# A recording list scheduler with new queue costs, other warm-up matmuls, and scanned states stored with the chunk innermost

## The chip, the cores and the metric

The kernel runs on one core of one Trainium2 chip. The metric is the device time of one execution in microseconds (us), as the median of several runs. Times inside an execution come from one profiled run.

## The reference

Three blocks follow each other, all in float32 with an output of 4 x 768 x 384. The first is a gated linear attention with a decaying state, the second mixes tokens with two 768 x 768 matrices after a rotation, the third is a gated spatial unit.

```python
f = 1.0 / (1.0 + np.exp(-f_logit))
for t in range(S):
    state = f[:, :, t, :, None] * state + np.einsum('bhd,bhe->bhde', k[:, :, t], v[:, :, t])
    y[:, :, t] = np.einsum('bhd,bhde->bhe', q[:, :, t], state)
...
theta = x @ w_theta
zr, zi = x * np.cos(theta), x * np.sin(theta)
y = np.einsum('ts,bsd->btd', w_tok_r, zr) + np.einsum('ts,bsd->btd', w_tok_i, zi)
u = x + y
x = u + np.maximum(u @ w_ch, 0.0)
...
h = np.maximum(x @ w_in, 0.0)
u, v = h[..., :512], h[..., 512:]
v_n = (v - mean(v)) / np.sqrt(var(v) + 1e-06)
out = (u * (np.einsum('ts,bsd->btd', w_spatial, v_n) + b_spatial[None, :, None])) @ w_out
```

There are 4 batches of 8 heads; a head has 768 steps and 48 channels.

## The kernel before

**The attention** takes two heads at a time: a unit u is one batch's pair of heads, 16 units in all, four for each batch. A head's 768 steps are cut into 12 chunks of 64. For a third of a batch's channels `dense` (line 462) loads f, k and q as tiles of 128 channels x 768 steps, makes the running decay `icp` with a scan on VectorE, and scales k and q with it; there are 12 such thirds. The tile f has one buffer, k and q have two (BUFS, line 39), so the load of the next f waits for the scan of the last. `att_load` (505) moves a unit's k and q rows within the chip into KP and QA, and loads v from HBM into VN and, straight behind q's rows, into VS. `att_k` (494) transposes k on TensorE (tile pt) and ScalarE copies it to KT. `att_s` (551) makes the 64 x 64 scores of six chunks (tile psc), which VectorE masks into QA. `att_w` (527) makes each chunk's own state (tile pw); ScalarE copies it to ub (called cu for the first four units), VectorE scans over the chunks in cb, with the chunk innermost, and ScalarE copies the states before each chunk to VS. VS is stored with the channel innermost, so both of these copies write one element in every 12 or 48. `att_x` (571) multiplies QA (stationary) with VS (moving, 48 columns) into px, which ScalarE copies to X.

**The mixing** transposes X (`p1_xt`), makes theta (`p1_theta`, tile pth), sine and cosine (`p1_z`), accumulates over the token matrices (`p1_acc`, tile acc) and applies the channel matrix (`p1_h`, tile hh). The first batch's matrices come as float64: `single` (394) loads the words of a block to ws (two buffers), and ScalarE and VectorE make float32 of them: w_theta into ft, the channel matrix into wb and wc, the token matrices into tk. **The third block** (`p2_v`, `p2_u`, `p2_s`, `p2_o`) follows batch by batch.

**The order.** Up to the third block every instruction is recorded by `Eng` (325; the profile therefore shows line 333 for all of them), and `Plan` (86) sets the order on each engine: `schedule` (197) runs a list schedule with `cost` (95) for each instruction, and for a DMA an issue time and a transfer at one rate; it repeats this four times with priorities from latest starts, keeps the best, and binds the order of TensorE, VectorE, ScalarE, GpSimd (POOL) and the one DMA queue, SP. SP issues in order: a DMA that waits for its data holds those behind it. The estimates set the order alone; waits are by semaphores. On TensorE all matmuls of one `group` stand together.

**Warm-up.** `run` (1013) issues FILL = 10 identity matmuls at the start; `warm` (426) adds two matmuls of 128 columns, whose result nobody reads, behind each bank of transposes and of scores in the first batch (12 transposes' and 16 scores' fillers).

Of the kernel before, what the change touches and what calls it, by code (L numbers as in the profile page):

```python
# [10 lines left out]
F32 = mybir.dt.float32  # L11
# [28 lines left out]

FILL = 10

# [11 lines left out]

MODE, HOP, ISSUE, RATE, LAND, SLACK = 0.1, 0.11, 0.45, 330e3, 0.9, 0.05
ROUNDS = 4
# [29 lines left out]
class Plan:  # L86
# [8 lines left out]
    def cost(self, o, e, ins, out, src):  # L95
        n = max([b.n for b in out + src] or [0])
        k = type(ins).__name__
        if e == "A":
            if k == "InstActivation":
                return 0.19 + 0.84e-3 * n + (0.95e-3 * n if abs(out[0].step) > 4 and n > 100 else 0)  # L100
            return 1.28
        if e == "V":
            if o.name.startswith("tensor_tensor_scan"):
                return 0.16 + 2.07e-3 * n
            if o.name == "tensor_scalar":
                return 0.15 + 0.53e-3 * n
            if o.name == "reciprocal":
                return 0.22
            return 0.15 + 1.045e-3 * n
        if e == "G":  # L110
            return 0.1 + 0.8e-3 * n if o.name == "memset" else 0.8
        if e == "Q":
            return ISSUE
        m, r = out[0].rows, out[0].n
        o.mode = (src[-1].rows, m)
        if o.name == "transpose":
            return 0.109
        if src[0].dt == F32R:
            return max(r / 2.4 + 13.3, m / 1.2 + 2) / 1e3
        if m < P:  # L120
            return max(2 * r / 2.4, 54) / 1e3 + 0.004
        return max(2 * (2 * r / 2.4 + 2), 214) / 1e3

    def add(self, e, name, ins):
# [5 lines left out]
        o.cost = self.cost(o, e, ins, o.out, o.src)  # L130
        o.bytes = max([b.n * b.rows * 4 for b in o.out] or [0])
        o.blk = (self.blk if e == "T" and self.blk else -o.i) if e == "T" else None
        o.pri = o.i if self.pri is None else self.pri
# [63 lines left out]
    def schedule(self):  # L197
# [30 lines left out]
        for _ in self.units:  # L228
# [21 lines left out]
            for o in u:  # L250
# [15 lines left out]
                elif e == "Q":  # L266
                    t += o.cost
                    dma = max(dma, t + 0.5) + o.bytes / RATE
                    end[o] = dma + LAND
                else:  # L270
                    if o.func == "sin":
                        t += 0.1 + (1.28 if func != "sin" else 0)
                    func = o.func or func
                    t += o.cost
                    end[o] = t + HOP
# [78 lines left out]
class Kernel:  # L354
    def __init__(self, tc, a):
        self.tc, self.a, self.nc = tc, a, tc.nc
        nc = tc.nc
        self.last, self.ready = None, False
        self.tk, self.nb, self.xt = {}, B, []
        self.cold = True  # L360
        self.plan = Plan(tc)
        e = {"V": nc.vector, "A": nc.scalar, "G": nc.gpsimd, "T": nc.tensor, "Q": nc.sync}
        self.V, self.A, self.G, self.T, self.Q = (Eng(self.plan, e[n], n) for n in "VAGTQ")
# [61 lines left out]

    def warm(self, p, src):
        if self.cold:
            for _ in range(2):
                self.T.matmul(p[:, DM:512], lhsT=src[:, 0:P], rhs=src[:, 0:P], start=True, stop=True)


    def att_open(self, ctx):
# [12 lines left out]
        self.cw = a1.tile([P, S], F32, name="cw")  # L445
        self.VS = [a1.tile([P, 2, NC, D], F32, name=f"vs{i}") for i in range(2)]
        self.VN = [a1.tile([P, 2, NT, D], F32, name=f"vn{i}") for i in range(2)]
# [8 lines left out]
        for t in self.VS:  # L456
            G.memset(t[0:64, 0, 0, :], 0.0)
            G.memset(t[64:128, 1, 0, :], 0.0)
        self.dn, self.un = {}, {}
# [34 lines left out]
    def att_k(self, b, g):  # L494
        self.group()
        k = self.dn[3 * b + g]["k"]
        for n in range(0, NT, 3):
            p = self.bank("pt")
            for i in range(3):
                self.T.transpose(p[:, P * i : P * i + P], k[:, P * (n + i) : P * (n + i) + P], self.ident)  # L500
            self.warm(p, k)
            self.A.activation(self.KT[:, n : n + 3, P * g : P * g + P], p[:, 0:DM].rearrange("p (n d) -> p n d", n=3), AF.Copy)
# [24 lines left out]
    def att_w(self, u):  # L527
# [9 lines left out]
        A.activation(cb, self.KP[w2][:, None, S:].to_broadcast([P, D, NC]), AF.Copy)  # L537
        w = [self.bank("pw")[:, 0 : 6 * D].rearrange("p (n d) -> p n d", n=NT) for _ in range(2)]
        for n in range(NT):
# [3 lines left out]
        for s in range(2):  # L543
            A.activation(ub[:, :, s:NC:2].rearrange("p e c -> p c e"), w[s], AF.Copy)
        fl = lambda z: z.rearrange("p e c -> p (e c)")
        V.tensor_tensor_scan(fl(cb), fl(ub), fl(cb), 0.0, op0=ALU.add, op1=ALU.mult)
        for i in range(2):
            r = slice(64 * i, 64 * i + 64)
            A.activation(VS[r, i, 1:NC, :].rearrange("p c e -> p e c"), cb[r, :, 0 : NC - 1], AF.Copy)

    def att_s(self, u, g):
        self.group()
        V, T = self.V, self.T
        K, qa = self.KP[u % 2], self.QA[u % 2]
        ps = self.bank("psc")
        for c in range(6):
            cc = slice(C * (6 * g + c), C * (6 * g + c) + C)
            for i in range(2):
                r = slice(64 * i, 64 * i + 64)
                T.matmul(ps[64 - 64 * i : 128 - 64 * i, C * c : C * c + C], lhsT=K[r, cc], rhs=qa[i][r, cc], start=True, stop=True)  # L560
        self.warm(ps, K)
        for i in range(2):
# [8 lines left out]
    def att_x(self, u, g, X):  # L571
        self.group()
        A, T, pr = self.A, self.T, u % NP
        qa, VS = self.QA[u % 2], self.VS[u % 2]
        ps = self.bank("px")[:, 0 : 6 * D].rearrange("p (n i d) -> p n i d", n=3, i=2)
        for i in range(2):
            for c in range(6):
                cc = 6 * g + c
                T.matmul(ps[64 * (c % 2) : 64 * (c % 2) + 64, c // 2, i, :], lhsT=qa[i][:, C * cc : C * cc + C], rhs=VS[:, i, cc, :], start=True, stop=True)
        A.activation(X[:, 3 * g : 3 * g + 3, 96 * pr : 96 * pr + 96].rearrange("p b (i e) -> p b i e", i=2), ps, AF.Copy)  # L580
# [42 lines left out]
    def p1_xt(self, b, X, tb):  # L623
# [4 lines left out]
        xt = self.xt[-1][:, :, P * (tb % 3) : P * (tb % 3) + P]  # L628
        p = self.mm.tile([P, 512], F32, name="pt", tag="th", bufs=2)
        for j in range(NJ):  # L630
            T.transpose(p[:, P * j : P * j + P], X[:, tb, P * j : P * j + P], self.ident)
# [8 lines left out]
    def p1_theta(self, b, tb, terms):  # L640
        self.group()
        V, A = self.V, self.A
        p = self.mm.tile([P, 512], F32, name="pth", tag="th", bufs=2)[:, 0:DM]
        (self.mm1 if b < THETA1 else self.mm3)(p, terms)
        sn = self.c2.tile([P, 2, DM], F32, name="sn", tag="sn")
# [226 lines left out]
    def general(self, xg, x2):  # L872
# [9 lines left out]
        with tc.For_i(0, B * NP, 1) as i:  # L882
            self.last, self.ready, self.cold = None, False, False
            f, k, q = [g1.tile([P, S], F32, name=f"g{n}") for n in "fkq"]
# [128 lines left out]
    def run(self):  # L1013
# [36 lines left out]
        run(w)  # L1050
        self.cold = False
        sw = ExitStack()
# [47 lines left out]
def layout(inputs):  # L1100
# [5 lines left out]
    def heads(x):  # L1106
# [12 lines left out]
        "vu": c(v2.reshape(B * NP, 2, NT, P, D).transpose(0, 3, 1, 2, 4)),  # L1119
        "va": c(v2.reshape(B * NP, 2, NC, C, D).transpose(0, 1, 3, 2, 4)),  # L1120
        "wt": raw(c(inputs["moe_w_theta"])),
# [21 lines left out]
```

## Time and profile before

| | us |
|---|---|
| median of 3 runs | 670.17 (665.01 to 672.14) |
| the profiled execution | 669.65 |
| its span | 667.5 |
| TensorE matmul busy | 611.6 (92%) |
| VectorE busy | 425.6 (64%) |
| ScalarE busy | 360.5 (54%) |
| GpSimd busy | 31.4 (5%) |

The profiled execution lasts 2.15 us longer than its span, which runs from the first to the last recorded work. PE is TensorE, PEld its weight loads, DVE VectorE, ACT ScalarE, SP the DMA queue. A float32 matmul leaves two records, a float32r matmul one. A busy PE is not a PE at its peak: ends are modelled, and a record counts as busy at either clock.

### The profile page before, as it was taken

The page shows a single profiled execution, that of the slowest core. Times are in us where ns is not written, and L with a number is a line of the kernel's source. Part 1 is how long each engine was busy: PE and PEld are TensorE (multiplying, and loading weights), DVE is VectorE, ACT ScalarE, POOL GpSimd, SP SyncE. Part 2 cuts the span into 40 slices and gives each one's busy share as a digit, 9 for nine tenths or more (in the row PEclk, how much of TensorE's full clock was granted, in tenths as well). Part 3 has the DMA queues.
Part 4 walks back from the last instruction along what each step waited for, and adds up shares of the span by engine and source line. Part 5 has one row for each costly group of instructions (what it writes and reads, how often), then busy time and mean ns, then how long its engine had stood idle before and what let it go on. Part 6 is the DMA issues. An engine that isn't in the chain of part 4 may idle for free.

```text
span 667.5 us, 12718 instructions
## 1 busy us (share of the span) xinstructions
PE 611.6 (92%) x5116; PEld 560.2 (84%) x5116; DVE 425.6 (64%) x757; ACT 360.5 (54%) x637; POOL 31.4 (5%) x72
## 2 busy tenths in 40 slices
PE   4468898599999799999999999999999999999996
PEld 4467566486789798898899998999899989998996
DVE  3786698688787796786588534769355354517250
ACT  3676788654886766895578211644362255126211
POOL 5110001000001020000000000000000000000000
PEclk7778998689999899999999999999999999999999
DMA  8876854878857979536565953341102000010002
GB/s 266 207 211 207 268 188 156 251 251 259 306 161 233 304 211 302 184 126 208 183 202 176 303 190 89 112 130 38 72 0 72 36 35 25 1 66 7 1 1 76
DMA packets 40962, 102.04 MB, mean 153 GB/s; under 512 B 5696, under 2 KB 11840, under 8 KB 40896
## 3 DMA queue, kind: packets, MB, share of 16 engines
q1 hardware_dynamic: 40896, 101.15, 48.1%
q8 instruction: 42, 0.69, 0.4%
q14 instruction: 24, 0.20, 0.1%
HBM read 71.17 MB, written 20.45 MB: 137 GB/s over the span
## 4 chain that ended last, share of the span: by engine, by line
PE 63%; DMA 16%; DVE 8%; ACT 6%; issue 3%; SPq 2%; POOL 1%; ACTq 0%; DVEq 0%; POOLq 0%
PE acc L333 14%; PE pg L333 14%; PE po L333 7%; PE pu L333 6%; PE pv L333 6%; PE pth L333 5%; DMA qa<-q 3%; PE hh L333 3%; DMA ws<-tok_dram 3%; PE psc L333 3%; DMA wb<-wp_dram 3%; PE px L333 2%; PE pt L333 2%; SPq L333 2%; DVE icp L333 2%
## 5 line engine op out<-in xcount | busy, mean ns | idle before, releaser
L333 PE MATMUL acc<-tk,z 128*128 128x384 f32 x828 | 169.0, 356 | 0.0
L333 PEld LDWEIGHTS acc<-tk,z 128*128 128x128 f32 x828 | 144.2, 189 | 9.6
L333 PE MATMUL pg<-wp,vn 128*128 128x384 f32 x576 | 101.0, 335 | 0.7 <-ACT wp L333 0.7
L333 PEld LDWEIGHTS pg<-wp,vn 128*128 128x128 f32 x576 | 99.9, 188 | 1.3 <-ACT wp L333 1.3
L333 PEld LDWEIGHTS psc<-qa,kp 64*64 64x64 f32 x768 | 31.5, 159 | 25.7 <-issue 21.3
L333 PE MATMUL psc<-qa,kp 64*64 64x64 f32 x768 | 35.9, 249 | 18.2 <-DMA qa<-q 11.6
L333 ACT ACTIVATE gt<-g 128x384 fp32r<-128x384 f32 x32 | 16.8, 526 | 63.6 <-DVE g L333 63.6
L333 PE MATMUL pu<-x,wi 128*128 128x384 f32 x288 | 50.7, 334 | 0.0
L333 PE MATMUL po<-wo,gt 128*128 128x384 f32 x288 | 50.6, 336 | 0.0
L333 PEld LDWEIGHTS pu<-x,wi 128*128 128x128 f32 x288 | 50.1, 188 | 0.3
L333 PEld LDWEIGHTS po<-wo,gt 128*128 128x128 f32 x288 | 50.0, 188 | 0.0
L333 PE MATMUL pv<-wi,x 128*128 128x512 f32 x216 | 49.8, 390 | 0.0
L333 DVE TENSOR_TENSOR qa<-psc,mask 64x384 f32<-64x384 f32 x64 | 35.5, 555 | 21.2 <-PE psc L333 19.9
L333 PEld LDWEIGHTS pv<-wi,x 128*128 128x128 f32 x216 | 40.5, 188 | 8.2
L333 PE MATMUL hh<-uT,wc 128*128 128x384 f32 x216 | 41.8, 343 | 2.3 <-DVE sn L333 1.0
L333 DVE BATCH_NORM_STATS2 st<-vv 128x6 f32<-128x512 f32 x24 | 16.5, 691 | 42.4 <-ACT vv L333 42.4
L333 PEld LDWEIGHTS px<-vs,qa 128*64 128x64 f32 x768 | 28.6, 156 | 16.0 <-ACT vs L333 7.9
L333 PE MATMUL px<-vs,qa 128*64 128x48 f32 x768 | 31.6, 242 | 10.8 <-ACT vs L333 7.1
L333 PEld LDWEIGHTS hh<-uT,wc 128*128 128x128 f32 x216 | 37.1, 188 | 4.6 <-DVE sn L333 1.4
L333 ACT ACTIVATE ws<-ws 128x768 f32<-128x768 f32 (+2 forms) x28 | 20.3, 732 | 28.6 <-DMA ws<-wi_dram 11.7
L333 DVE TENSOR_TENSOR g<-pg,bs 128x384 f32<-128x384 f32 x32 | 17.7, 555 | 27.2 <-PE pg L333 27.2
L333 ACT ACTIVATE vs<-cb 64x528 f32<-64x528 f32 x24 | 27.7, 1154 | 11.5 <-DVE cb L333 11.3
(113 smaller groups left out, 938.1 us busy)
## 6 DMA issues: line engine op xcount, KB each, us to landing
tk<-tkp SPq DMA_DIRECT2D x48, 384.0 KB, 4.3
ws<-tok_dram SPq DMA_DIRECT2D x12, 768.0 KB, 6.5
tkp<-tk SPq DMA_DIRECT2D x20, 384.0 KB, 4.5
f<-f_dram SPq DMA_DIRECT2D x12, 384.0 KB, 4.8
k<-k_dram SPq DMA_DIRECT2D x12, 384.0 KB, 5.2
q<-q_dram SPq DMA_DIRECT2D x12, 384.0 KB, 6.2
vn<-vu_dram SPq DMA_DIRECT2D x16, 288.0 KB, 5.0
vs<-va_dram SPq DMA_DIRECT2D x32, 144.0 KB, 4.2
```

What stands on the lines that cost most here:

```text
L333: r = f(*a, **k)
```

## The change

Four things. The planner's DMA costs: issue 0.6 us (was 0.45), 310 GB/s (was 330), 160 GB/s for transfers to 96 partitions or fewer, 1.2 us to land (was 0.9). The fillers: 30 at the start and 20 ahead of the first scores, all identity matmuls, which the planner counts as free; the 28 of the first batch's transposes and scores are gone. VS is stored as channel by chunk, with the chunk innermost, so the two copies follow the scan's own order and `att_x` reads a moving operand with a step of 12 elements; v's copy in HBM is laid out to match. The planner's extra cost for strided copies on ScalarE is gone.

```diff
-FILL = 10
+FILL = 30
+WARM = {("s", 0, 0): 20}
...
-MODE, HOP, ISSUE, RATE, LAND, SLACK = 0.1, 0.11, 0.45, 330e3, 0.9, 0.05
+MODE, HOP, ISSUE, RATE, NARROW, LAND, SLACK = 0.1, 0.11, 0.6, 310e3, 160e3, 1.2, 0.05
...
-                return 0.19 + 0.84e-3 * n + (0.95e-3 * n if abs(out[0].step) > 4 and n > 100 else 0)
+                return 0.19 + 0.84e-3 * n
...
+        if len(src) == 2 and src[0].t == src[1].t:
+            return 0.0
...
+        o.rate = RATE if max([b.rows for b in o.out] or [P]) > 96 else NARROW
...
-                    dma = max(dma, t + 0.5) + o.bytes / RATE
+                    dma = max(dma, t + 0.5) + o.bytes / o.rate
...
-    def warm(self, p, src):
-        if self.cold:
-            for _ in range(2):
-                self.T.matmul(p[:, DM:512], lhsT=src[:, 0:P], rhs=src[:, 0:P], start=True, stop=True)
+    def warm(self, p, key):
+        for _ in range(WARM.get(key, 0)):
+            self.T.matmul(p[:, 0:P], lhsT=self.ident, rhs=self.ident, start=True, stop=True)
...
-        self.VS = [a1.tile([P, 2, NC, D], F32, name=f"vs{i}") for i in range(2)]
+        self.VS = [a1.tile([P, 2, D, NC], F32, name=f"vs{i}") for i in range(2)]
...
-            G.memset(t[0:64, 0, 0, :], 0.0)
-            G.memset(t[64:128, 1, 0, :], 0.0)
+            G.memset(t[0:64, 0, :, 0], 0.0)
+            G.memset(t[64:128, 1, :, 0], 0.0)
...
-            A.activation(ub[:, :, s:NC:2].rearrange("p e c -> p c e"), w[s], AF.Copy)
+            A.activation(ub[:, :, s:NC:2], w[s].rearrange("p n e -> p e n"), AF.Copy)
...
-            A.activation(VS[r, i, 1:NC, :].rearrange("p c e -> p e c"), cb[r, :, 0 : NC - 1], AF.Copy)
+            A.activation(VS[r, i, :, 1:NC], cb[r, :, 0 : NC - 1], AF.Copy)
...
-                T.matmul(ps[...], lhsT=qa[i][:, C * cc : C * cc + C], rhs=VS[:, i, cc, :], start=True, stop=True)
+                T.matmul(ps[...], lhsT=qa[i][:, C * cc : C * cc + C], rhs=VS[:, i, :, cc], start=True, stop=True)
...
-        "va": c(v2.reshape(B * NP, 2, NC, C, D).transpose(0, 1, 3, 2, 4)),
+        "va": c(v2.reshape(B * NP, 2, NC, C, D).transpose(0, 1, 3, 4, 2)),
```

The order changes at many places. The first shown is SP from the second load of f to the third. In names like f1 or k2 the digit is the third of the channels; in kp0, qa00, qa01 it is the buffer and the head of a unit; ws is a raw weight block. Before:

```order
L333 DMA f1_205<-f_dram 128x768
L333 DMA qa01_107<-q0_142 48x768
L333 DMA kp0_104<-k0_140 48x780 x2
L333 DMA qa00_106<-q0_142 48x768
L333 DMA kp1_105<-k0_140 32x780
L333 DMA qa10_108<-q0_142 32x768
L333 DMA ws_174<-wt_dram 128x768
L333 DMA ws_828<-wc_dram 128x768
L333 DMA k2_344<-k_dram 128x768
L333 DMA q2_346<-q_dram 128x768
L333 DMA f2_342<-f_dram 128x768
```

The same place in the change:

```order
L337 DMA f1_221<-f_dram 128x768
L337 DMA qa00_106<-q0_142 48x768
L337 DMA ws_174<-wt_dram 128x768
L337 DMA kp0_104<-k0_140 48x780 x2
L337 DMA qa01_107<-q0_142 48x768
L337 DMA kp1_105<-k0_140 32x780
L337 DMA qa10_108<-q0_142 32x768
L337 DMA ws_840<-wc_dram 128x768
L337 DMA f2_370<-f_dram 128x768
L337 DMA k2_372<-k_dram 128x768
L337 DMA q2_374<-q_dram 128x768
```

The third f moves ahead of the third k and q, and the weight block ws_174 moves ahead of the first unit's kp0 and qa01.

The second place is VectorE, from the scan over the first unit's chunks (cu0) to the third decay scan (icp from f2). Before:

```order
L333 SCALAR_TENSOR_TENSOR cu0_250<-cu0_250 128x576
L333 TENSOR_TENSOR q1_209<-q1_209,cw_99 128x768
L333 TENSOR_TENSOR qa00_106<-psc_283,mask_91 64x384
L333 TENSOR_TENSOR qa01_107<-psc_283,mask_91 64x384
L333 TENSOR_SCALAR ft2_173<-ws_174 128x384
L333 SCALAR_TENSOR_TENSOR ft2_173<-ws_174,ft2_173 128x384 x2
L333 TENSOR_SCALAR wb_827<-ws_828 128x384
L333 SCALAR_TENSOR_TENSOR wb_827<-ws_828,wb_827 128x384
L333 RECIPROCAL fs2_348<-f2_342 128x12
L333 SCALAR_TENSOR_TENSOR wb_827<-ws_828,wb_827 128x384
L333 SCALAR_TENSOR_TENSOR icp_98<-f2_342,one_95 128x768
```

In the change:

```order
L337 TENSOR_TENSOR k1_223<-k1_223,icp_98 128x768
L337 TENSOR_TENSOR icp_98<-cw_99,icp_98 128x768
L337 SCALAR_TENSOR_TENSOR cw_99<-icp_98,cw_99 128x768
L337 TENSOR_TENSOR q1_225<-q1_225,cw_99 128x768
L337 TENSOR_TENSOR qa00_106<-psc_249,mask_91 64x384
L337 TENSOR_TENSOR qa01_107<-psc_249,mask_91 64x384
L337 SCALAR_TENSOR_TENSOR cu0_284<-cu0_284 128x576
L337 TENSOR_TENSOR qa00_106<-psc_317,mask_91 64x384
L337 TENSOR_TENSOR qa01_107<-psc_317,mask_91 64x384
L337 RECIPROCAL fs2_376<-f2_370 128x12
L337 TENSOR_SCALAR wb_839<-ws_840 128x384
L337 SCALAR_TENSOR_TENSOR icp_98<-f2_370,one_95 128x768
```

Two steps of the weight conversion wb go behind the third decay scan, and the k and q of the second third go ahead of the unit's masks and scan.

The third place is TensorE at the sixth unit (kp_105, vs_101) in the second batch's attention, at the end of its scores. Before:

```order
L333 MATMUL psc<-qa_109,kp_105 64x64
L333 MATMUL pt<-ident,k_1008 128x128 x6
L333 MATMUL px<-vs_101,qa_108 64x48 x6
L333 MATMUL px<-vs_101,qa_109 64x48 x6
L333 MATMUL px<-vs_101,qa_108 64x48 x6
L333 MATMUL px<-vs_101,qa_109 64x48 x6
L333 MATMUL pw<-vn_102,kt 64x48 x24
L333 MATMUL psc<-qa_106,kp_104 64x64
```

In the change:

```order
L337 MATMUL psc<-qa_109,kp_105 64x64
L337 MATMUL pt<-ident,k_1020 128x128 x6
L337 MATMUL acc<-tk_1158,z_834 128x384
L337 MATMUL acc<-tk_1159,z_834 128x384
L337 MATMUL acc<-tk_1158,z_835 128x384
L337 MATMUL acc<-tk_1158,z_834 128x384
L337 MATMUL acc<-tk_1159,z_834 128x384
L337 MATMUL acc<-tk_1158,z_835 128x384
L337 MATMUL px<-vs_101,qa_108 64x48 x6
L337 MATMUL px<-vs_101,qa_109 64x48 x6
L337 MATMUL px<-vs_101,qa_108 64x48 x6
L337 MATMUL px<-vs_101,qa_109 64x48 x6
```

Six of the first batch's acc matmuls stand ahead of px, and twelve more follow between pw and the next scores, where before none stood.

## Rows read from the trace of the kernel before

**Rows 1.** Windows: stretch, length, busy of each engine, PEclk, DMA share, GB/s.

```profile
21.12:34.29 13.17, 8.89 (x158) 7.96 (x159) 11.59 (x18) 9.09 (x14) 2.33 (x4) 0.76 0.74 215
34.29:46.55 12.26, 7.28 (x128) 6.21 (x126) 10.26 (x15) 8.77 (x15) 1.35 (x4) 0.78 0.87 261
46.55:65.90 19.35, 16.69 (x296) 15.04 (x294) 13.32 (x18) 12.09 (x19) 2.16 (x3) 0.74 0.59 189
65.90:105.12 39.22, 35.71 (x272) 24.13 (x268) 30.16 (x46) 31.50 (x55) 0.12 (x1) 0.96 0.68 214
...
105.00:137.00 32.00, 21.04 (x302) 18.48 (x300) 24.65 (x28) 19.70 (x30) 3.50 (x8) 0.71 0.74 218
150.00:440.00 290.00, 281.07 (x2523) 257.45 (x2521) 206.67 (x339) 182.53 (x317) 12.80 (x25) 0.99 0.65 206
```

**Rows 2.** Timeline of the opening: start, length, engine, what, count.

```profile
21.12 1.75 DVE L333 TENSOR_TENSOR_SCAN icp<-f,one 128x768 f32<-128x768 f32 x1
...
23.54 0.42 SPq L333 DMA_DIRECT2D f<-f_dram  x1
...
29.47 2.26 ACT L333 ACTIVATE vs<-cu 64x528 f32<-64x528 f32 x2 [1.02 <-DVE cu L333]
...
31.76 1.72 ACT L333 ACTIVATE f<-f 128x768 f32<-128x768 f32 x2
...
34.29 1.75 DVE L333 TENSOR_TENSOR_SCAN icp<-f,one 128x768 f32<-128x768 f32 x1
...
46.55 1.74 DVE L333 TENSOR_TENSOR_SCAN icp<-f,one 128x768 f32<-128x768 f32 x1
...
65.90 0.54 DVE L333 TENSOR_SCALAR tk<-ws 128x768 uint32<-128x768 uint32 x1
...
66.60 1.95 PE L333 MATMUL px<-vs,qa 128*64 128x48 f32 x58 [0.59 <-ACT vs L333]
```

**Rows 3.** The chain that ended last: start, length, engine, what.

```profile
16.90 5.32 DMA qa<-q
...
37.08 5.82 DMA f<-f_dram
...
125.07 8.37 DMA qa<-q
...
231.33 0.84 PE psc L333 x24
...
234.47 0.84 PE pw L333 x48
235.32 3.32 PE acc L333 x18
...
239.48 1.54 PE px L333 x48
```

**Rows 4.** Groups by form: shapes, count, busy us, mean ns, idle before.

```profile
L333 ACT ACTIVATE vs<-cb 64x528 f32<-64x528 f32 x24 | 27.7, 1154 | 11.5 <-DVE cb L333 11.3
...
L333 ACT ACTIVATE ub<-pw 128x288 f32<-128x288 f32 x24 | 14.6, 704 | 2.4 <-PE pw L333 2.4
...
L333 ACT ACTIVATE X<-px 128x288 f32<-128x288 f32 x32 | 12.4, 402 | 3.3 <-PE px L333 3.1
...
L333 DVE SCALAR_TENSOR_TENSOR wb<-ws,wb 128x384 uint32<-128x384 uint32 x14 | 7.7, 546 | 0.2
...
L333 PE MATMUL psc<-kp 128*128 128x128 f32 x32 | 6.7, 341 | 0.0
...
L333 PE MATMUL pt<-k 128*128 128x128 f32 x24 | 6.4, 420 | 0.0
...
L333 PE MATMUL pt<-ident 128*128 128x128 f32 x20 | 4.4, 413 | 1.5 <-POOL ident masks.py:199 1.5
...
L333 POOL MEMSET f<- 128x12 f32 x12 | 1.7, 140 | 187.1 <-DVE fs L333 187.0
...
L333 POOL MEMSET vs<- 64x48 f32 x4 | 0.5, 132 | 0.2
```

More of the change, by code (lines that the diff above doesn't have):

```diff
@@ L359, in __init__ @@
         self.tk, self.nb, self.xt = {}, B, []
-        self.cold = True
         self.plan = Plan(tc)
@@ L498, in att_k @@
             p = self.bank("pt")
+            self.warm(p, ("k", b, g, n))
             for i in range(3):
                 self.T.transpose(p[:, P * i : P * i + P], k[:, P * (n + i) : P * (n + i) + P], self.ident)
-            self.warm(p, k)
             self.A.activation(self.KT[:, n : n + 3, P * g : P * g + P], p[:, 0:DM].rearrange("p (n d) -> p n d", n=3), AF.Copy)
@@ L537, in att_w @@
         A.activation(cb, self.KP[w2][:, None, S:].to_broadcast([P, D, NC]), AF.Copy)
-        w = [self.bank("pw")[:, 0 : 6 * D].rearrange("p (n d) -> p n d", n=NT) for _ in range(2)]
+        w = [self.bank("pw") for _ in range(2)]
+        self.warm(w[0], ("w", u))
+        w = [x[:, 0 : 6 * D].rearrange("p (n d) -> p n d", n=NT) for x in w]
         for n in range(NT):
@@ L555, in att_s @@
         ps = self.bank("psc")
+        self.warm(ps, ("s", u, g))
         for c in range(6):
@@ L560, in att_s @@
                 T.matmul(ps[64 - 64 * i : 128 - 64 * i, C * c : C * c + C], lhsT=K[r, cc], rhs=qa[i][r, cc], start=True, stop=True)
-        self.warm(ps, K)
         for i in range(2):
@@ L574, in att_x @@
         qa, VS = self.QA[u % 2], self.VS[u % 2]
-        ps = self.bank("px")[:, 0 : 6 * D].rearrange("p (n i d) -> p n i d", n=3, i=2)
+        ps = self.bank("px")
+        self.warm(ps, ("x", u, g))
+        ps = ps[:, 0 : 6 * D].rearrange("p (n i d) -> p n i d", n=3, i=2)
         for i in range(2):
@@ L578, in att_x @@
                 cc = 6 * g + c
-                T.matmul(ps[64 * (c % 2) : 64 * (c % 2) + 64, c // 2, i, :], lhsT=qa[i][:, C * cc : C * cc + C], rhs=VS[:, i, cc, :], start=True, stop=True)
+                T.matmul(ps[64 * (c % 2) : 64 * (c % 2) + 64, c // 2, i, :], lhsT=qa[i][:, C * cc : C * cc + C], rhs=VS[:, i, :, cc], start=True, stop=True)
         A.activation(X[:, 3 * g : 3 * g + 3, 96 * pr : 96 * pr + 96].rearrange("p b (i e) -> p b i e", i=2), ps, AF.Copy)
@@ L629, in p1_xt @@
         p = self.mm.tile([P, 512], F32, name="pt", tag="th", bufs=2)
+        self.warm(p, ("t", b, tb))
         for j in range(NJ):
@@ L643, in p1_theta @@
         p = self.mm.tile([P, 512], F32, name="pth", tag="th", bufs=2)[:, 0:DM]
+        self.warm(p, ("z", b, tb))
         (self.mm1 if b < THETA1 else self.mm3)(p, terms)
@@ L882, in general @@
         with tc.For_i(0, B * NP, 1) as i:
-            self.last, self.ready, self.cold = None, False, False
+            self.last, self.ready = None, False
             f, k, q = [g1.tile([P, S], F32, name=f"g{n}") for n in "fkq"]
@@ L1050, in run @@
         run(w)
-        self.cold = False
         sw = ExitStack()
```

## The prediction, made before the change was run

> **What bounds the kernel now.** I read the windows by stage first, then the timeline of the opening, the chain that ended last, and the groups by form. From 150 to 440 us TensorE is busy for 281.07 of 290 us at a granted clock of 0.99 [rows 1]: nine microseconds are to be had there, whatever other engines do. The change can win in the first 137 us. There the clock is 0.71 to 0.78 in four stretches of five, a mixture of the levels 1.2 and 2.4 GHz, and VectorE is the fullest engine: 11.59 of 13.17 us, 10.26 of 12.26, then 13.32 of 19.35 [rows 1]. I cut these stretches at the decay scans at 21.12, 34.29 and 46.55 and at the first token block's conversion (tk) at 65.90 [rows 2], since each scan needs the f whose load waits for the scan before: f was issued at 23.54, and ScalarE took it up at 31.76, after two vs copies of 2.26 us that began at 29.47 [rows 2]. The fourth f landed 5.82 us after 37.08, and the chain that ended last goes through this load and through loads of qa of 5.32 and 8.37 us [rows 3]. So the opening is a loop of loads, ScalarE and VectorE, and TensorE waits for it.
>
> **The change part by part.** All times are of the profiled execution, 669.65 us, which is 0.5 below the median of 670.17.
>
> *Copies.* A vs copy takes 1154 ns [rows 4]. Without the step I take it from two contiguous copies: 402 ns for 288 elements (X) [rows 4] and 1.72 / 2 = 0.86 us for 768 (f) [rows 2], so about 0.63 us for 528: 0.52 saved, 32 times, 16.8 us of ScalarE. The ub copies take 704 ns against the 402 of X with the same size [rows 4]. They now write with a step of two and read PSUM with a step of 48; no row shows such a read, so they end between 402 and 704; I take the middle, 0.15 saved, 32 times. Of all this only what lies in the first 137 us counts, as ScalarE is busy for only 182.53 of 290 us in the dense stage, beside a TensorE that is nearly full [rows 1].
>
> *From the second scan to the third.* Between them VectorE has the same work as before but for two wb steps of 546 ns [rows 4], which go behind the third scan: 11.59 - 1.09 = 10.5 us. Its idle time there, 1.58 us, I expect to shrink to 1.0: f is now loaded ahead of k and q and taken by ScalarE ahead of the vs copies. The third scan comes at 21.1 + 10.5 + 1.0 = 32.6, 1.7 us earlier. Against it: the weight block ws_174 now waits on SP for a VectorE step, with kp0, qa01 and four more behind it, and TensorE's first scores wait for those. Its 384 KB are 1.8 us at the stretch's 215 GB/s [rows 1]; qa landed at 16.90 + 5.32 = 22.2 [rows 3], so the scores start at about 24. VectorE's masks stand behind k, icp, cw and q now and are due at 28: 4 us of cover for scores that need under 3 us. I take nothing; without the cover it costs 1.8.
>
> *To the fourth scan.* VectorE has 10.26 us of work [rows 1], and about 0.2 more, as two wb steps replace one and a short one: 32.6 + 10.5 = 43.1. The fourth f has one weight block fewer ahead of it and the queue reaches it 0.6 us sooner: it lands near 40.6 in place of 42.9, and 1.72 of ScalarE and 0.6 of small steps lead to 43.0. I take 43.5, 3.0 earlier than 46.55 [rows 2].
>
> *To the token block.* VectorE's work is 13.32 [rows 1], plus a wb conversion less one step, 0.9: the conversion of tk cannot begin before 43.5 + 14.2 = 57.7, and was at 65.90. The idle 6 us were waits for scores, which hang on px, on the vs copies of two units (4 x 0.52 = 2.1 us shorter) and on the fillers that go: 6.7 + 6.4 = 13.1 us of TensorE over the opening [rows 4]. I let 1.5 us of idle time stay: 59.2, which is **6.7 us** earlier, with 0 and 8.2 as ends. The last px of the first batch, at 66.60 + 1.95 = 68.6 [rows 2], should then end near 60.
>
> *65.90 to 137.* VectorE has 30.16 and ScalarE 31.50 of 39.22 us [rows 1], with one unit's copies shorter by 2 x 0.52 + 2 x 0.15 = 1.3. I take **1.0** more won, between 0 and 4. From 105 to 137 TensorE works 21.04 of 32 us [rows 1] and waits for qa. Eighteen acc matmuls, 3.32 us when they follow each other [rows 3], move from behind this wait into it, but the same queue must bring the loads: **1.0**, between a loss of 2 and a gain of 4.
>
> *Fillers.* Twenty records of the opening's fillers took 4.4 us [rows 4], so sixty take 13.2 and end at 14.7. Transposes take 1.3, and forty more records 8.4 to 10.6 us, by 6.7 / 32 and 6.4 / 24 [rows 4]. They end at 24.4 to 26.6, at or behind the scores' start near 24. The cover is that of the first scores above; I take nothing, and 2.6 as the other end. The removed fillers may leave the clock lower in the opening; TensorE waits there, so nothing, with 3 as the other end.
>
> *GpSimd.* Four memsets of vs, 132 ns each, stand ahead of the memset that the first scan waits for; they now step 48 bytes. The memset of f with a step takes 140 ns for only 12 elements, the 48 contiguous ones 132 [rows 4]. The ends are 0 and 4 x 0.4 = 1.6, if time went with the count; I take **0.3** lost.
>
> *The moving operand of px.* No row shows a matmul with a step. px takes 1.54 us for 48 records, psc 0.84 for 24, pw 0.84 for 48 [rows 3]. psc runs on two parts of the array at a time, pw on four, px on two: a step of 70, 70 and 64 ns per record and part. psc streams 64 columns and pw 48, at one step, so 16 columns' time is spare in pw, and px is of its width. From the other side: a stepped element cost ScalarE (704 - 402) / 288 = 1.05 ns more [rows 4]; 48 of them are 50 ns per record, and 384 records in a row on each part 19.4 us; were the parts to share, 38.7. The nearest rows are TensorE's own; I take 0, and keep 19.4 as the end.
>
> The row that speaks against the change is ScalarE's: 704 ns for a write with a step and 402 without [rows 4]. The Trainium skill, "SBUF — State Buffer", Specifications (TRN2), says that a line is 16 bytes and that full bandwidth needs two hits on it; px's new elements lie 48 bytes apart, one to a line. By that rule px would slow down, and the sum would be the first rival's; by psc and pw it stays as it is.
>
> The sum: -6.7 - 1.0 - 1.0 + 0.3 = -8.4, which gives 661.25 by the profiled execution and 661.8 by the median. I forecast **661.5**.
>
> **The rivals.**
> *TensorE pays for the step.* The opening gains as above, and each px record takes 50 ns more. Three quarters of the units lie behind 105 us, most of them in the dense stage, where nothing hides it: 288 x 50 ns = 14.4 us, and half of the first four units' 4.8: 17 us, 678. For it: ScalarE's row, and a TensorE busy for 281 of 290 us. Against: psc and pw at one step. It turns the gain into a loss from 8.4 us / 384 = 22 ns per record, a px of 2.1 us in place of 1.54.
> *The gain is given back in the queue.* The first batch ends earlier, but token blocks, f, k, q and qa come through one queue, with DMA busy for 0.87, 0.68 and 0.74 in the stretches [rows 1], and an 8.37 us qa load stands in the chain [rows 3]. If the 65.90 to 137 stretches stretch by 5 us, 666.5. Against: the queue is idle for 0.41 of the stretch before [rows 1].
> *The new order does not do what it says.* If the masks that go behind k and q hold up the first units as much as the f loop gains, the token block moves by 2 us, and the time is 667. It is counted with the second.
>
> **How the numbers follow.** The forecast has 0.50 with a range of its own of 656 to 667, given back or not gained 0.30, the step 0.20. A change of 1% is about what a measurement of this kernel can tell: 663.5 and 676.9. Faster by more: 0.42 of the first, 0.05 of the second and 0.03 of the third case, with a step of a few ns: 0.50. Slower by more: 0.12, nearly all from the third. The rest, 0.38, lies within. The range takes the end of 8.2 in place of 6.7 and the gains of 4 for 1.0 twice: 661.5 - 7.5 = 654; above it reaches into the third case, to 676.
>
> **What would show it.** Right: the decay scans near 32.6 and 43.5, tk converted from about 59, the last px of the first batch near 60, vs copies at 0.63 us, px at 1.54 us per unit on the full clock. Wrong: px above 2 us there; or a first token block before 60 and yet TensorE entering the third block less than 4 us earlier, with longer loads of qa or tk between; or the first scores behind fillers, past 27 us.

## The result, and the profile after

| | before | after |
|---|---|---|
| median of five runs of each on one chip, us | 668.76 (665.01 to 672.14) | 652.64 (647.52 to 655.39) |
| ratio of times, 95% interval | | 0.976 (0.9721 to 0.9799) |
| the profiled execution, us | 669.65 | 647.52 |
| its span, us | 667.5 | 645.5 |

The change gained 16 us, 2.4%, where 8.4 were forecast; 652.64 lies under the range. The profiled execution of after is the fastest of its five, so the stages below show 22 us, some 6 more than the medians do.

The windows of after, cut where the program stands at the same point as before: at the first conversion of tk, at the scan of the second batch's first f, at the first store of a token result (x2d) and at the first pv of the third block. Columns as in [rows 1]; the last row answers to the last of [rows 1].

```profile
0.00:59.23 59.23, 40.65 (x666) 37.87 (x668) 44.40 (x62) 34.47 (x58) 14.06 (x39) 0.83 0.82 251
59.23:95.52 36.29, 33.86 (x244) 22.80 (x240) 31.19 (x49) 30.32 (x54) 0.12 (x1) 1.00 0.64 212
95.52:139.51 43.99, 37.61 (x522) 31.34 (x524) 39.28 (x51) 25.80 (x43) 3.98 (x9) 0.81 0.82 263
139.51:390.62 251.11, 248.85 (x2350) 230.62 (x2349) 182.74 (x275) 153.61 (x275) 8.23 (x23) 1.00 0.69 221
390.62:645.00 254.38, 249.12 (x1369) 240.24 (x1368) 128.56 (x324) 95.69 (x207) 0.00 (x0) 1.00 0.15 49
150.00:440.00 290.00, 287.74 (x2539) 270.34 (x2538) 212.78 (x359) 176.16 (x324) 7.99 (x21) 1.00 0.64 202
```

The kernel before at the same five points (its second stage stands in [rows 1]):

```profile
0.00:65.90 65.90, 40.50 (x612) 36.36 (x612) 43.68 (x61) 38.35 (x56) 15.08 (x39) 0.74 0.77 225
...
105.12:156.98 51.86, 40.40 (x545) 33.69 (x545) 40.98 (x54) 30.83 (x46) 3.53 (x8) 0.80 0.74 226
156.98:410.88 253.90, 245.38 (x2327) 225.82 (x2325) 182.20 (x274) 163.93 (x276) 12.68 (x24) 0.99 0.67 215
410.88:667.00 256.12, 249.66 (x1369) 240.18 (x1368) 128.62 (x324) 95.90 (x207) 0.00 (x0) 0.99 0.15 49
```

Read them as an account of TensorE: length less busy time is its idle time. In total it is busy for as long as before, 610.1 against 611.7 us; fillers count as busy, 14.5 us of them in after (9.9 and 4.6, below) and 17.5 in before (4.4, 6.7 and 6.4 [rows 4]). The idle time went from 25.4 to 18.6 in the opening, from 3.5 to 2.4 to the second batch, from 11.5 to 6.4 to the first store, from 8.5 to 2.3 in the dense stage, and from 6.5 to 5.3 behind it: 20.4 of the 22 us. Two thirds of that, 13.6, lie behind the opening. By length the opening is 6.7 us shorter, and the stretches behind it 2.9, 7.9, 2.8 and 1.7.

The timeline of the opening, as in [rows 2]:

```profile
13.78 2.96 PE L337 MATMUL psc<-ident 128*128 128x128 f32 x25
...
19.97 1.76 DVE L337 TENSOR_TENSOR_SCAN icp<-f,one 128x768 f32<-128x768 f32 x1 [0.27 <-POOL f L337]
...
21.75 0.33 SPq L337 DMA_DIRECT2D f<-f_dram  x1
22.28 0.44 PE L337 MATMUL psc<-qa,kp 64*64 64x64 f32 x2 [5.54 <-DMA kp<-k]
...
27.28 1.71 ACT L337 ACTIVATE f<-f 128x768 f32<-128x768 f32 x2
30.50 1.31 ACT L337 ACTIVATE vs<-cu 64x528 f32<-64x528 f32 x2 [1.51 <-DVE cu L337]
32.09 1.76 DVE L337 TENSOR_TENSOR_SCAN icp<-f,one 128x768 f32<-128x768 f32 x1
...
43.42 1.74 DVE L337 TENSOR_TENSOR_SCAN icp<-f,one 128x768 f32<-128x768 f32 x1
...
56.91 3.85 PE L337 MATMUL px<-vs,qa 128*64 128x48 f32 x72 [0.80 <-PE px L337]
...
59.23 0.55 DVE L337 TENSOR_SCALAR tk<-ws 128x768 uint32<-128x768 uint32 x1
```

The fillers end at 13.78 + 2.96 = 16.74, and TensorE then waits 5.54 us for kp. The third f is issued ahead of the third k and q, ScalarE takes it ahead of the vs copies, and the scans come at 32.09 and 43.42, tk at 59.23, and the last px of the first batch ends at 56.91 + 3.85 = 60.8.

The groups by form, as in [rows 4]:

```profile
L337 PE MATMUL px<-vs,qa 128*64 128x48 f32 x768 | 40.6, 275 | 7.3 <-ACT vs L337 5.9 <-PE px L337 0.8 <-DVE qa L337 0.5
L337 ACT ACTIVATE vs<-cb 64x528 f32<-64x528 f32 x24 | 15.4, 642 | 4.7 <-DVE cb L337 4.5
...
L337 PE MATMUL pt<-ident 128*128 128x128 f32 x60 | 9.9, 346 | 1.5 <-POOL ident masks.py:199 1.5
...
L337 ACT ACTIVATE ub<-pw 128x288 f32<-128x288 f32 x24 | 9.1, 427 | 1.9 <-PE pw L337 1.8
...
L337 PE MATMUL psc<-ident 128*128 128x128 f32 x40 | 4.6, 275 | 0.0
...
L337 POOL MEMSET vs<- 64x48 f32 x4 | 0.7, 176 | 0.2
```

The chain that ended last: its shares by engine, in before and in after, then pieces of after that answer to [rows 3].

```profile
PE 63%; DMA 16%; DVE 8%; ACT 6%; issue 3%; SPq 2%; POOL 1%; ACTq 0%; DVEq 0%; POOLq 0%
```

```profile
PE 82%; DVE 8%; DMA 3%; ACT 2%; POOL 1%; issue 1%; SPq 1%; ACTq 0%; DVEq 0%; POOLq 0%
...
17.06 5.57 DMA kp<-k
35.95 4.36 DMA f<-f_dram
...
106.07 3.22 DMA qa<-q
...
127.70 2.22 PE px L337 x48
...
195.30 6.39 DMA vn<-vu_dram
```

Loads are 3% of the chain where they were 16%. The 8.37 us load of qa is gone; the longest load left in it is one of vn, 6.39 us. One unit's px takes 2.22 us where it took 1.54 [rows 3].

### The profile page after: what moved, and what is told of

Read it like the earlier page. It is cut to its first block, busy times and chain, and to the rows that moved or that the text cites. A ratio compares the mean times of both kernels' runs of the same rounds, so it can differ in the third digit from the quotient of the medians.

```text
span 645.5 us, 12790 instructions
## 1 busy us (share of the span) xinstructions
PE 610.1 (95%) x5140; PEld 562.9 (87%) x5140; DVE 426.2 (66%) x757; ACT 339.9 (53%) x637; POOL 26.4 (4%) x72
## 4 chain that ended last, share of the span: by engine, by line
PE 82%; DVE 8%; DMA 3%; ACT 2%; POOL 1%; issue 1%; SPq 1%; ACTq 0%; DVEq 0%; POOLq 0%
PE acc L337 20%; PE pg L337 15%; PE pu L337 8%; PE po L337 8%; PE pv L337 8%; PE px L337 6%; PE hh L337 6%; PE pth L337 5%; PE psc L337 3%; PE pt L337 2%; PE pw L337 1%; DVE tk L337 1%; DVE icp L337 1%; DVE sn L337 1%; DVE qa L337 1%
## 5 line engine op out<-in xcount | busy, mean ns | idle before, releaser
L337 PEld LDWEIGHTS acc<-tk,z 128*128 128x128 f32 x828 | 144.4, 190 | 11.2 <-DVE tk L337 1.6
L337 PEld LDWEIGHTS px<-vs,qa 128*64 128x64 f32 x768 | 36.5, 170 | 12.8 <-ACT vs L337 6.4
L337 PE MATMUL px<-vs,qa 128*64 128x48 f32 x768 | 40.6, 275 | 7.3 <-ACT vs L337 5.9
L337 PEld LDWEIGHTS psc<-qa,kp 64*64 64x64 f32 x768 | 27.8, 145 | 19.0 <-issue 10.1
L337 PE MATMUL psc<-qa,kp 64*64 64x64 f32 x768 | 31.6, 233 | 13.1 <-DMA kp<-k 5.5
L337 ACT ACTIVATE X<-px 128x288 f32<-128x288 f32 x32 | 13.1, 409 | 30.6 <-PE px L337 30.4
```

What stands on the lines that cost most here:

```text
L337: r = f(*a, **k)
```

## The experiments

Theory A: the order that the queue's numbers make is the gain. Theory B: the shorter copies are. Theory C: the fillers warm TensorE. Theory P came up after the first four runs: a plan is a draw, any change of a planner number throwing the order anew. "Order" is that of the instructions on each engine.

| | queue numbers | layout of states | fillers | us, median | ratio to before, 95% |
|---|---|---|---|---|---|
| e1 | new | old, order as after | new | 655.29 | 0.9763 to 0.9891 |
| e2 | new | old for vs, order as after | new | 648.88 | 0.9693 to 0.979 |
| e3 | old | new | new | 679.47 | 1.0113 to 1.0229 |
| e4 | old | new | old | 662.27 | 0.9897 to 0.9966 |
| e5 | new | old | old | 658.78 | 0.9821 to 0.9944 |
| e6 | new | new | old | 658.76 | 0.9806 to 0.9931 |
| e7 | new | new, order as after | none | 653.61 | 0.9711 to 0.985 |
| e9, e10 | half new | new | new | 658.1, 655.02 | 0.9818 to 0.9873, 0.975 to 0.983 |
| e11, e12 | new, one planner number moved | new | new | 659.84, 666.55 | 0.9858 to 0.9913, 0.9945 to 1.0008 |
| e13, e14 | old, the same number moved | new | new | 672.08, 665.59 | 1.0032 to 1.0084, 0.9944 to 1.0001 |
| e8, e16 | new | both, order as after | new | 646.03, 646.84 | 0.9653 to 0.9767, 0.9672 to 0.9747 |
| e15 | after once more | | | 650.94 | 0.9711 to 0.9777 |

**The layouts at one order.** e1 goes back to the states with the channel innermost, all instructions on all engines in after's order:

```diff
-        self.VS = [a1.tile([P, 2, D, NC], F32, ...
+        self.VS = [a1.tile([P, 2, NC, D], F32, ...
...
-            A.activation(ub[:, :, s:NC:2], w[s].rearrange("p n e -> p e n"), AF.Copy)
+            A.activation(ub[:, :, s:NC:2].rearrange("p e c -> p c e"), w[s], AF.Copy)
...
-            A.activation(VS[r, i, :, 1:NC], cb[r, :, 0 : NC - 1], AF.Copy)
+            A.activation(VS[r, i, 1:NC, :].rearrange("p c e -> p e c"), cb[r, :, 0 : NC - 1], AF.Copy)
...
```

> The change with the states stored as before (channel innermost; ub and vs copies write with a step, px reads 48 contiguous elements), and with the same order of instructions on all five engines as the change, so that only durations differ. px should go back from 2.23 to 1.54 us per unit (11 us of TensorE in 16 units), vs copies from 0.64 to 1.15 us and ub copies from 0.43 to 0.70 (25 us of ScalarE). Theory A (the gain is the new order, and px's step costs what it adds to TensorE): 652.6 - 8 + 2 = 647. Theory B (the shorter copies, on the way from scan to px, make the gain): 658 or more, with longer waits of px for vs.

Measured 655.29, between the two: some twelve of the sixteen us are there with the old layout, by the order and the new fillers; e7 below finds the fillers worth nothing, so this is the order's. At after's order the new layout adds 2.7 to 4.4 us (against 652.64 and 650.94) by the medians; the intervals of the ratios overlap.

e2 keeps after's ub copies, stores VS with the channel innermost, and moves the step from the write of the vs copy to its read:

```diff
...
-            A.activation(VS[r, i, :, 1:NC], cb[r, :, 0 : NC - 1], AF.Copy)
+            A.activation(VS[r, i, 1:NC, :], cb[r, :, 0 : NC - 1].rearrange("p e c -> p c e"), AF.Copy)
...
```

> The change with the states stored channel innermost again and px contiguous, but the vs copies write in the stored order and read the scan's tile with a step of 12; ub as in the change; same order on all engines. If a stepped read costs ScalarE as little as it does from PSUM (ub 0.427 against 0.402 us for X), vs copies stay near 0.65 us, px is 1.54 us, and the time falls by about 8 us to 644 to 645. If reads cost what writes cost, vs copies are 1.15 us and the time is that of e1 less what ub saves.

```profile
L337 PE MATMUL px<-vs,qa 128*64 128x48 f32 x768 | 34.7, 251 | 10.7 <-ACT vs L337 9.6 <-DVE qa L337 1.1
L337 ACT ACTIVATE vs<-cb 64x528 f32<-64x528 f32 x24 | 27.7, 1156 | 4.7 <-DVE cb L337 4.4
...
L337 ACT ACTIVATE ub<-pw 128x288 f32<-128x288 f32 x24 | 9.1, 427 | 3.3 <-PE pw L337 3.2
```

In these groups of e2 a read with a step costs the vs copy as much as a write did, 1156 ns against 642, while ub's read of PSUM, 427, is nearly that of the contiguous X. So e2 differs from e1 in price by the ub copies alone, 0.28 us each (711 ns in e1), 32 times, 9.1 us of ScalarE, and is 6.4 us faster; its slowest run (650.83) lies under e1's fastest (651.25). From e2 to after the vs copies save 32 x 0.51 = 16.4 us of ScalarE, TensorE pays for px, and the median is 2 to 4 us longer, which the spread of the runs covers. Over the whole kernel, the half of the layout that pays is ub's; by stages the vs copies pay too, in the opening, as the last table of this section shows.

e4 puts the new layout alone into the kernel before.

> The kernel before with the states stored chunk innermost and nothing else (the planner sees the shorter copies by itself; order planned anew). Theory A: px adds 11 us of TensorE, some of it in waits, the copies save less: 670 to 676. Theory B: 656 to 660.

662.27 meets neither; it is 0.7% under before, in an order that is new as well, since ScalarE's costs enter the plan.

**The queue's numbers.** e3 takes the four numbers back in the changed kernel (0.45, 330e3, 0.9, no narrow rate), e5 puts the new ones alone into the kernel before.

> The change with the planner's four DMA costs as before (0.45, 330, no lower rate for narrow transfers, 0.9), so the order is planned anew. Theory A: most of the gain goes, 661 to 666. Theory B: it stays near 653 to 656.

> The kernel before with the planner's queue numbers alone (0.6 us an issue, 310e3, 160e3 for narrow transfers, 1.2 us to land); states, copies and fillers stay as before. Theory A (the order that the queue's numbers make is the gain, about 14 us of it): 655 to 658. Theory B (the shorter copies are the gain): 664 or more, as the copies keep their 1.15 us. Theory P (each number that enters the planner throws the order anew, and single parts don't add up): anything between 650 and 682, and not what the sum of the other steps gives.

e5's 658.78 is just past A's bound and has ten of the sixteen us with copies of 1.15 us. But e3 at 679.47 is slower than before, and 17 us slower than e4, which differs by its fillers (and by the planner's costs of them and of stepped copies). No sum of parts gives that: the parts do not add up.

**The fillers.** e6 has before's fillers, in an order of its own; e7 takes out 49 of after's 50 and leaves the order.

> The changed kernel with the fillers of before (10 at the start, two behind each of the first transposes and score groups). Theory A: the fillers do little, 650 to 655. Theory C (the 50 identity products at the start warm TensorE and are worth several us): 657 or more, the granted clock before the 35th us lower than the changed kernel's 0.80. Theory P: the order is thrown anew, 640 to 680.

> The changed kernel without its 29 + 20 fillers, every other instruction of TensorE, VectorE, ScalarE and the queues of the opening and the dense stage in the same order. Theory A: 652 to 654, no difference from the changed kernel. Theory C: 657 or more, because TensorE's granted clock up to 60 us falls below the changed kernel's 0.83; a fall to 0.73 would cost 0.1 of some 35 us of its work there, 3.5 us, where that is waited for.

e7's 653.61 lies 1.0 us over after's 652.64 and 2.7 over e15's 650.94, the intervals overlapping, so as work the fillers count for nothing that these runs can tell. The granted clock to 35 us is higher without them, 1.00 in e7 against 0.80 in after (the last column but two), which is the opposite of C; e7 first:

```profile
0.00:35.00 35.00, 10.45 (x153) 9.06 (x154) 21.58 (x30) 16.30 (x25) 11.02 (x33) 1.00 0.83 240
```

```profile
0.00:35.00 35.00, 24.19 (x255) 23.13 (x256) 22.44 (x31) 16.53 (x26) 11.75 (x33) 0.80 0.82 243
```

e6 alone would have passed for C: 658.76, and a clock of 0.71 to 35 us. But e7 contradicts C, and e4, with the same fillers as e6, shows 1.00 there. That leaves e6's order as the likely cause; no run tries it apart.

**Is a plan a draw?** e9 takes only the narrow rate back, e10 keeps only it. e11 writes 305e3 for 310e3 and e12 0.12 for 0.11 us from engine to engine, neither nearer to the trace. e13 and e14 make these two moves (330e3 to 325e3; 0.11 to 0.12) in e3.

> The changed kernel, but the planner gives narrow transfers the rate of wide ones (310e3 for 160e3); issue 0.6, landing 1.2 as in the changed kernel. Theory A (the queue's numbers that fit the trace better make the gain, each its part): the narrow value loads are four in the opening, 653 to 660. Theory P (a plan is a draw: any change of a number throws the order anew, and the time is anywhere from 647 to 680): outside of 653 to 660 in one of these four runs at least.

> The changed kernel with the planner's old issue, rate and landing (0.45, 330e3, 0.9), but 160e3 for narrow transfers. Theory A: between the run with the old numbers (679.5) and the changed kernel, 655 to 672, above the run without the narrow rate. Theory P: no order among the two halves; may be below 653 or above 672.

> The changed kernel with the planner's rate 305e3 for 310e3, a change of 1.6% that fits the trace neither better nor worse. Theory A: 650 to 655, as the changed kernel. Theory P: off by 4 or more, 647 or 657 to 680.

> The changed kernel with the planner's time from an engine's end to the next engine's start 0.12 for 0.11 us, nothing to do with the queue. Theory A: 650 to 655, as the changed kernel. Theory P: off by 4 or more, 647 or 657 to 680.

> The changed kernel with the old queue numbers (as the run that gave 679.5), but the rate 325e3 for 330e3, 1.5% lower. Theory A (new numbers gain on average, each plan a draw around it): 662 to 676, mean of the three draws with old numbers some 8 to 12 above the mean of the three with new ones (652.6, 659.8, 666.6: mean 659.7). Theory P (the numbers' size carries nothing, only the draw): 650 to 664, so that the means come within 5 of each other.

> The changed kernel with the old queue numbers and the time between engines 0.12 for 0.11 us. Theory A: 662 to 676. Theory P: 650 to 664.

e12 lost 14 us by 0.01 us in a table, e11 7. That is P, and e12 is the one outside 653 to 660 that it asked for. But e9, e10, e13 and e14 all lie in the ranges that A gave, and e13 and e14 above P's; of these four A misses only in that e10 is not slower than e9. Its 650 to 655 for e11 and e12 failed. Either half of the new numbers, e9 or e10, brings 21 or 24 of the 27 us from e3 to after. The three plans with old numbers average 672.4, with new ones 659.7 (652.64, 659.84, 666.55), but the pairs differ by 26.8, 12.2 and -1.0. With the pairs that have the old fillers, e4 to e6 (3.5) and before to e5 (10.0), the mean is 10 with a spread of 11, so its error is 5, two errors from zero. What the numbers are worth on average is likely some ten us, and not settled; that one plan differs from the next by as much is shown.

What the numbers do in all these plans is in the waits. TensorE's waits between 59 and 400 us in after (waited for: us in total, times, longest):

```profile
PE pt L337 <- DVE k L337: 4.4, 1, 4.4
PE psc L337 <- DMA qa<-q: 1.8, 1, 1.8
PE psc L337 <- DVE qa L337: 1.5, 1, 1.5
PE acc L337 <- DVE tk L337: 1.2, 1, 1.2
```

The longest of the same in e14, with the old numbers, where one load of qa holds it for 11 us:

```profile
PE psc L336 <- DMA qa<-q: 11.0, 1, 11.0
PE pth L336 <- ACT xt L336: 4.4, 1, 4.4
```

And in e12, with the new ones, where loads are short and VectorE and ScalarE are late instead:

```profile
PE pt L337 <- DVE k L337: 6.3, 1, 6.3
PE hh L337 <- DVE sn L337: 4.2, 1, 4.2
PE pth L337 <- ACT xt L337: 3.2, 2, 2.3
```

Summing all such rows by what was waited for:

| us, 59 to 400 | old numbers: before, e3, e13, e14, e4 | new numbers: after, e11, e12, e5, e6 |
|---|---|---|
| for a DMA | 4.1, 10.6, 7.2, 14.1, 5.8 | 1.8, 0.9, 3.7, 0.9, 2.8 |
| for VectorE and ScalarE | 17.2, 19.7, 18.1, 10.4, 14.1 | 9.2, 19.0, 21.6, 19.5, 14.2 |

Every plan with the new numbers waits less for loads than every plan with the old, by 6.3 us in the mean: this much of A is real, though it rests on one trace of each plan, and the nearest two, before and e12, are 0.4 apart (a second trace of after's plan, e15, has 0.9 for after's 1.8). The half plans e9 and e10 have 2.7 and 2.5. The second row has no such order, and there after is the lowest of all ten, its second trace with 11.0 the third lowest of eleven. That part of its gain is its draw.

The windows of e12, cut at the same scan and the same first pv (after's stretch between them is 295.10 long, with 286.45 busy):

```profile
0.00:94.12 94.12, 72.61 (x886) 58.84 (x886) 71.15 (x103) 62.28 (x108) 15.18 (x40) 0.85 0.79 227
94.12:409.20 315.08, 294.13 (x2886) 270.05 (x2887) 226.56 (x330) 183.48 (x323) 14.11 (x32) 0.95 0.67 216
```

e12 reaches the second batch 1.4 us ahead of after and then takes 20 us longer to the third block: 12.3 of it is idle time of TensorE, 21.0 us against 8.7, and the rest is busy time, at a granted clock of 0.95 against 0.97. A good opening does not make a good dense stage.

**A version with both layouts.** e8 uses each layout where it should pay: chunk innermost for the first batch, whose scans wait for copies; channel innermost with a stepped read for the other twelve units, where TensorE is full.

```diff
+    def states(self, t, u):
+        if u < NP:
+            return t.rearrange("p i (e c) -> p i e c", c=NC)
+        return t.rearrange("p i (c e) -> p i e c", c=NC)
...
+            if u >= NP:
+                o, c = o.rearrange("p e c -> p c e"), c.rearrange("p e c -> p c e")
+            A.activation(o, c, AF.Copy)
...
```

> The changed kernel with the chunk innermost for the first batch's four units alone; the other twelve have the channel innermost, copied through a stepped read, so TensorE streams their states packed; four small clears on GpSimd more. Theory A (up to 60 us the copy is waited for, behind it TensorE's products are): the opening keeps the changed kernel's scans (32.1, 43.4) and the dense stage gains what TensorE saves, 12 units of 0.69 us less what the copies cost there: 645 to 650. Theory B (the copies are waited for throughout): 650 to 655.

> The changed kernel once more, as the measure for the next run in the same session: 650 to 655 by every theory.

> The kernel with two state layouts once more. If TensorE's products are what is waited for behind 60 us: 645 to 649 and its ratio at least 0.005 below the changed kernel's in the same session. If the layouts give no more than they take: the ratios within 0.003.

The chain of e8 has a unit of the first batch, with the step, and later ones without:

```profile
30.13 2.82 PE px L337 x46
...
115.86 2.73 PE px L337 x48
...
126.37 1.53 PE px L337 x48
```

In after, where all have the step, the chain has:

```profile
117.45 2.73 PE px L337 x48
...
213.40 2.23 PE px L337 x48
```

What the step costs hangs on the clock. In the windows of these pieces the granted clock is 0.50, that is 1.2 GHz, for 30.13, 115.86 and 117.45, and 1.00, 2.4 GHz, for 126.37 and 213.40. At the lower level a unit takes 2.73 us with the step or without; at the full one 2.23 with it and 1.53 without. So the twelve units save less than 12 x 0.69 = 8.3: px is busy for 40.6 us in after and 34.1 in e8, 6.5 less.

646.84 against 650.94 in one session is 4.1 us. The ratios differ by 0.0035, less than the 0.005 asked for, and their intervals overlap: likely faster, not settled.

The stages of all kernels with after's order, and of before, cut as in the section on the result (us, one execution each), show where each layout pays. A dear vs copy takes about 1.15 us and a cheap one 0.64, a dear ub copy 0.70 and a cheap one 0.43; "then" is behind the first batch:

| | vs copies | ub copies | px | to tk | to the second batch | to the first store | to the third block | span |
|---|---|---|---|---|---|---|---|---|
| before (old order) | dear | dear | packed | 65.90 | 39.22 | 51.86 | 253.90 | 667.5 |
| e1 | dear | dear | packed | 62.80 | 37.64 | 42.63 | 253.63 | 651.9 |
| e2 | dear | cheap | packed | 62.40 | 38.07 | 41.73 | 248.37 | 645.7 |
| after | cheap | cheap | stepped | 59.23 | 36.29 | 43.99 | 251.11 | 645.5 |
| e15 | cheap | cheap | stepped | 60.05 | 36.62 | 43.26 | 253.76 | 648.9 |
| e7, no fillers | cheap | cheap | stepped | 61.24 | 36.62 | 43.79 | 255.46 | 653.0 |
| e8 | cheap, then dear | cheap | stepped, then packed | 57.97 | 36.32 | 44.48 | 248.24 | 643.5 |
| e16 | cheap, then dear | cheap | stepped, then packed | 57.82 | 36.30 | 44.41 | 249.91 | 644.7 |

The cheap vs copies pay in the opening, 62.4 against 59.2 and 60.1; ub's cheap copies and a packed px pay in the dense stage, 253.6 against 248.2 to 249.9, and with px stepped that stage is 251.1 to 255.5. e8 has the better of both. One thing in it was not foreseen: its opening is 1.3 to 2.2 us shorter than after's in the same layout and order. Its first scores start at 20.35 (e16 20.65) for after's 22.28 (e15 22.02), behind a load of kp; why that load lands sooner is open, so not all of the 4.1 us is the layout's.

## Why the prediction was wrong

- *The opening* (-6.7): right in its times, and in part by luck. Third scan 32.6 forecast, 32.09 measured; fourth 43.5 and 43.42; tk 59.2 and 59.23 (60.05 in e15); the last px near 60 and 60.8. But the three stretches between were each longer than forecast, 12.1, 11.3 and 15.8 us for 11.5, 10.9 and 15.7; the second scan, which I had left at 21.12, came at 19.97 and covered it. Nor was VectorE the fullest engine throughout: from 46.55 to 65.90 TensorE, with fillers, had 16.69 us to its 13.32 [rows 1]. By e1, 3.1 of the 6.7 us are there with the old copies, and the rest came with the cheaper ones.
- *65.90 to 137* (-1.0 and -1.0): **the step that failed.** The stretch from tk to the second batch went from 39.22 to 36.29, and from there to the first store from 51.86 to 43.99: 10.8 won (11.2 in e15) where I took 2.0 for about the same ground, and kept 4 and 4 as ends. I priced it by the copies saved and by eighteen moved matmuls, and took the idle time there for a wait for qa. The copies are not it: e1, with the old ones in after's order, wins 10.8 here too. Nor was it mostly qa. TensorE's waits from 105.12 to 156.98 in before:

```profile
PE psc L333 <- DMA qa<-q: 3.7, 2, 2.1
PE pt L333 <- DVE k L333: 2.7, 1, 2.7
PE px L333 <- ACT kt L333: 2.0, 1, 2.0
PE pw L333 <- ACT X L333: 1.6, 1, 1.6
```

  Over both stretches TensorE waited 7.1 us for ScalarE, 4.2 for VectorE and 3.7 for loads in before, and 1.4, 5.6 and 1.8 in after. The new order thus took away waits for ScalarE above all, 5.7 us, and 1.9 for loads; the other 4.6 of the 10.8 is busy time, of which the same 192 score records account for 3.1 (10.8 us before, 7.7 after). Which of the moved instructions did it stays open.
- *The dense stage* (0, as "nine microseconds are to be had there" [rows 1]): near in size, by luck. Idle time there fell from 8.5 to 2.3 us, nearly all that was to be had and was taken as untouched, and TensorE's busy time rose by 3.5, as px pays its step there: the stage is 2.8 us shorter in after, and 0.1 in e15, with 3.15 idle. Two terms that I put at nothing nearly cancel. The third block behind it is 1.7 shorter.
- *px* (0, end 19.4): wrong in size, and the first rival's mechanism is true at the full clock. 2.23 less 1.54 is 0.69 us for a unit, 29 ns for each of 24 records on a part, over the break-even of 22 that I gave; at the lower clock it is nothing, so px as a whole is busy for 6.3 us more than in e1 at the same order (40.6 and 34.3). The dense stages of e2, e8 and e16 against those of after, e15 and e7 show that it is paid in time. The kernel is faster since the order's term above was larger, not since px was free. The comparison with psc and pw was no guide at the full clock; ScalarE's row, 50 ns, was a little nearer.
- *The Trainium skill's rule*, "SBUF — State Buffer", Specifications (TRN2), on two hits in a 16-byte line: the traces agree for ScalarE's reads and writes of SBUF (1156 and 1154 ns against 642) and for TensorE's moving operand at the full clock (2.23 us against 1.53), all dearer at 48 bytes from element to element; at the lower clock px shows no such price (2.73 both ways).
- *Copies*: vs 0.63 forecast, 0.642 measured; ub 0.55 as the middle, 0.427 measured, at the lower end, and by e1 and e2 it is the edit that pays.
- *Fillers* (0): right, for another reason. They ended not at 24.4 but at 16.74, since they took 9.9 and 4.6 us where I had 13.2 and 8.4, and TensorE then waited 5.54 us for kp.
- *GpSimd* (0.3): four memsets of 176 ns for 132, 0.18.
- *Given back in the queue*: false. TensorE's waits for loads are shorter in all five plans with the new numbers, and the 65.90 to 137 stretches shrank.

What I left out is that the change re-orders the whole program up to the third block. I priced the places whose order I had read, and took the rest as it was; two thirds of the gain came from behind the opening, 10.8 us of it from 65.90 to the first store, and e12 shows that it could as well have gone the other way.

## What to carry to other kernels

Where a planner sets the order, an edit to its costs is a new draw for every stage: price the idle time of each stage as what may go or double, not as zero, and give the range that width. Before such a gain is credited to the numbers, move another number by a hair and time three or four plans; keep the best by measurement. A layout step is paid by whoever reads or writes it, so put it on the engine that has time in that stage, or where it is cheap: here, ScalarE's read of PSUM, or TensorE while it runs at its lower clock. And trace the same plan twice before a stage's gain is explained: the dense stage's 2.8 us in one trace of this plan were 0.1 in the next.

## What the runs showed of the hardware

- A step of 48 bytes costs a ScalarE copy of 528 elements the same on the read of SBUF as on the write: 1156 and 1154 ns against 642. A step of 192 bytes on its read of PSUM costs almost nothing: 427 ns for 288 elements, against 409 for X.
- A moving operand with a step of 48 bytes costs TensorE 29 ns per float32 record of 48 columns at a granted clock of 1.00 (2.23 us for a unit against 1.53), and nothing at 0.50 (2.73 us in after with the step and in e8 without).
- The granted clock to 35 us was 1.00 without the fillers (e7) and 0.80 with them (after); with before's fillers it was 0.73 in before, 0.71 in e6 and 1.00 in e4. The scans behind came 0.9 to 1.3 us later without them (32.95 and 44.76 against 32.09 and 43.42), in one execution of each.
- Runs of one and the same plan lay up to 1.2% apart (647.52 to 655.39), more than many edits are worth.
